# Ends of attention units in pairs, in-place scaling, narrower masks and fused VectorE exponentials in a four-layer attention kernel

## The chip, the cores and the metric

One Trainium2 chip, one of its cores. The metric is the device time of the kernel in microseconds (us), the median of three runs. The engines are TensorE (PE in the profile; PEld is its weight load), VectorE (DVE), ScalarE (ACT), GpSimd (POOL) and SyncE (SP, which here only issues DMAs). PSUM is the memory that TensorE writes: eight banks of 128 x 512 float32.

## The reference, cut to what matters

Four layers on x of 2048 rows by 640 columns. Each normalizes x, projects it to queries, keys and values of 32 heads of 20 columns, and adds attention times an output matrix to x. Layers 0 and 2 (weights A) see a causal window of 256 keys, layers 1 and 3 (weights B) see all 2048 keys.

```python
scores = jnp.einsum("bhqd,bhkd->bhqk", q, k) * (Dh ** -0.5)
scores = jnp.where(mask[None, None], scores, -1e9)     # A: 0 <= q - k < 256; B: no mask
p = _softmax(scores, axis=-1)
o = jnp.einsum("bhqk,bhkd->bhqd", p, v)
...
x = x + _A_ref(_layernorm(x, axis=-1), A_wqkv, A_wo)   # layer 0, then B (1), A (2), B (3)
```

## The kernel before, in words

**Units, banks and tiles.** The queries are cut into four chunks c of 512 rows, the heads into eight groups g of four. A *unit* (layer l, c, g) is the attention of four heads for 512 queries. It consists of *banks*: the scores of one head for 128 keys by 512 queries, one PSUM bank each. A full unit has 16 x 4 = 64 banks, a windowed one 3 x 4 = 12, in which every bank combines parts of two key blocks under one of three masks. The first chunk's units of layers 1 and 3 are cut into parts by key blocks (PARTS, L43), so that they can begin before all keys exist.

**The loop (L1259).** Each turn is a *tile* and advances the planner's clock by one. It takes two to four banks; TensorE writes their scores (L1298) in PSUM banks 0 to 2 at even tiles and 3 to 5 (with 6 at times) at odd ones; ScalarE makes the exponentials of the whole tile in one instruction (L1329) into a tile `pt`; then come pending side tasks (`pump`, L1340), filler matmuls that keep TensorE busy (`keep_clock`, L1342; `unread`, L638, recorded at L640), and the products with the values for tiles two or three turns older (L1363), which accumulate in PSUM bank 7 (`op`). Behind them VectorE gets its share of exponentials (`side_step`, L1385) and the masking of the tile before (L1399): a multiplication by a 0/1 mask, over all 512 columns of a bank, or from the first written block on. Mask 1 has zeros only in the second and third 128 of its 512 columns.

**The side tasks** are generators for projections (L370, L471), layer norms (L394), outputs (`t_out`, L545, matmuls L558) and the units' ends. They are sorted by the unit that needs them; `require` runs them at once when something isn't there in time. Each of them borrows a spare PSUM bank (`take_m`, L269): banks 5 and 6 while tiles are narrow, bank 6 alone after that, at most one borrower a tile.

**A unit's end.** `finish_unit` (L840) copies `op` to a tile `oT` (L863, or L861 with the earlier parts added) and pushes a tail (`t_tail`, L1030), one a unit. Row 20 of each head's 32 rows holds the sum of the exponentials. The tail gathers these sums by four matmuls with a selector (L1044), takes reciprocals (L1049), splits them in two bf16 parts `hl` (L1053, L1054), transposes them on TensorE (L1061), copies that to `rT` (L1063), spreads it over the rows by four matmuls (L1072), and multiplies `oT` by it into the chunk's tile `on` (L1079). Each of the three steps with PSUM borrows the spare bank once. When g = 7 is done, the chunk's output is pushed.

**Packed outputs.** In layer 3 (`packed`, L129) the scaled rows go into one of three staging slots of `on` and are moved by DMAs on SP (L1090) into dense rows, so that the output takes five matmuls for each 128 x 320 block instead of eight. The two last units of the last chunk aren't packed. The output matrix is loaded accordingly, sparse or dense (`load_wop`, L133).

**VectorE's exponentials.** In layers 1 and 3, for c > 0 (two units excepted), the last key block of two heads (layer 1) or four heads (layer 3) is left to VectorE (`aside`, L685). `t_side` (L890) handles two banks as a pair: an eviction each (L911), then ten steps on 1024 columns (L916 to L949) that build 2^x from the bits of the float's exponent and a polynomial of its fraction. Every step has a charge (0.7 or 1.2), and each tile adds a credit (L1384): 1.05 (SIDE_RATE, L40) in the last stage, 0.65 before. A step is issued while the credit is above zero. In the last stage its scores (L904) go to bank 6, at odd tiles (L1266). If a unit closes earlier than its pairs, `side_need` (L980) and `side_done` (L996) force the rest out at once. The products of these banks with the values are L1372.

Of the kernel before, what the change touches and what calls it, by code (L numbers as in the profile page):

```python
# [34 lines left out]
EK, ES, EB, EC, ED = (  # L35
    0.34108128280528366, -0.013389613744261132, 0.7155463694844106,
    0.9531181402314826, 0.010462897723623632,
)
KA = 18
SIDE_RATE = 1.05  # L40
# [9 lines left out]
def kernel(  # L50
# [25 lines left out]
    otp = pool("otp", 3)  # L76
# [22 lines left out]
    spread4 = big.tile([32, 4, P], BF16, name="spread4", tag="spread4")  # L99
# [29 lines left out]
    def packed(l, c):  # L129

        return l > 2

    def load_wop(w, dense):  # L133
        if dense:
            nc.sync.dma_start(out=wop[:, 0:KD, :], in_=wo_in[w].rearrange("(b p) f -> p b f", p=P))
            if w and out_n[0] == 12:
                v = wo_in[w].rearrange("(g j e) f -> j e g f", g=G, j=4)
                for j in range(4):
                    nc.sync.dma_start(
                        out=wop[32 * j : 32 * j + DH, G - 2 : G, :], in_=v[j][:, G - 2 : G, :]  # L140
                    )
            return
        v = wo_in[w].rearrange("(g j e) f -> j e g f", g=G, j=4)
        for j in range(4):
            nc.sync.dma_start(out=wop[32 * j : 32 * j + DH, :, :], in_=v[j])
# [23 lines left out]
    def other_constants():  # L169
        nc.vector.memset(op, 0.0)  # L170
        nc.vector.tensor_copy(
            out=sel4[:], in_=ident[:].rearrange("p (j m) -> p j m", j=4)[:, :, DH]
        )

        sp32 = rzp.tile([32, 2, 16], BF16, name="sp32", tag="sp32")
        nc.vector.tensor_copy(
            out=sp32[:], in_=ident[0:32, 0:32].rearrange("p (n r) -> p n r", n=2)
        )
        sp16 = rzp.tile([32, 16], BF16, name="sp16", tag="sp16")
        nc.vector.tensor_tensor(out=sp16[:], in0=sp32[:, 0, :], in1=sp32[:, 1, :], op=ALU.add)  # L180
        nc.vector.tensor_copy(
            out=spread4[:].rearrange("p q (j m) -> p (q j) m", m=32),
            in_=sp16[:].unsqueeze(2).to_broadcast((32, 16, 32)),
        )
# [360 lines left out]
    def t_out(l, c):  # L545
# [32 lines left out]
        if n < len(out_seq) and (n == 12 or out_seq[n] != out_seq[n - 1]):  # L578
            load_wop(out_seq[n], n >= 12)
# [260 lines left out]
    def finish_unit(u):  # L840
        l, c, g = u.l, u.c, u.g
        if u.part and u.part[1] < NT:
            if not part_o:
                part_o["t"] = big.tile([P, G, C], F32, name="raw_o", tag="early_late")
            raw_o = part_o["t"][:, g, :]
            if u.part[0] == 0:
                nc.vector.tensor_copy(out=raw_o, in_=op)
            else:
                nc.vector.tensor_tensor(out=raw_o, in0=raw_o, in1=op, op=ALU.add)
            return  # L850
        if (l, c) not in ons:
            for ll, cc in list(ons):
                if len(ons) >= 2:
                    require(("out", ll, cc))
            ons[l, c] = onp.tile([P, G, C], BF16, name="on", tag="on")
        on = ons[l, c]
        while len(tails) >= 3:
            require(("tail", *tails[0].name[1:]))
        oT = otp.tile([P, C], BF16, name="oT", tag="oT")
        if u.part:  # L860
            nc.vector.tensor_tensor(out=oT[:], in0=part_o["t"][:, g, :], in1=op, op=ALU.add)  # L861
        else:
            nc.vector.tensor_copy(out=oT[:], in_=op)  # L863
        push_tail(("tail", l, c, g), t_tail(l, c, g, on, oT))


# [4 lines left out]
    def side_start():  # L871

        assert live["xnT"] == 0
        tl = [xtp.tile([P, KD, C], BF16, name="xnT", tag="xnT") for _ in range(4)]
        live["xnT"] += 4
        f = [v[:, 0:4, :].rearrange("p a b -> p (a b)") for v in tl[0:3]]
        side["tiles"] = [v.bitcast(F32) for v in f] + [tl[3][:, 0:2, :].rearrange("p a b -> p (a b)")]
        side["out"] = deque(ka_all[:, KA - 6 + 2 * n : KA - 4 + 2 * n, :] for n in range(3))
        side["late"] = True

    def side_early():

        b = part_o["t"]
        side["tiles"] = [b[:, 2 * n : 2 * n + 2, :].rearrange("p a b -> p (a b)") for n in range(3)]
        side["tiles"].append(b[:, 6, :].bitcast(BF16))
        side["out"] = deque([b[:, 7, :].bitcast(BF16).rearrange("p (a b) -> p a b", a=2)])
        side["gen"] = t_side()
        side_step(False)

    def t_side():  # L890

        V = nc.vector
        while aside:
            u = aside[0]
            for pair in range(len(u.aside) // 2):
                while id(u) not in loaded or (u.l == 3 and not side["late"]):
                    yield None
                for i in range(2):
                    yield "bank"
                    xi, xm, xw, xe = side["tiles"]  # L900
                    if u.l == 3:
# [11 lines left out]
                        scalar1=SCALE * LOG2E * E23, scalar2=127.0 * E23, op0=ALU.mult, op1=ALU.add,  # L913
# [3 lines left out]
                    out=xm.bitcast(I32), in0=xi.bitcast(I32), scalar1=0x7FFFFF, scalar2=0x3F800000,  # L917
# [4 lines left out]
                    out=xi.bitcast(I32), in0=xi.bitcast(I32), scalar1=-0x800000, scalar2=None,  # L922
                    op0=ALU.bitwise_and,
                )
                yield 0.7
                V.tensor_scalar(out=xe, in0=xi, scalar1=0.0, scalar2=None, op0=ALU.max)
                yield 0.7
                V.tensor_scalar(
                    out=xm, in0=xm, scalar1=EK, scalar2=ES, op0=ALU.mult, op1=ALU.add
                )  # L930
                yield 0.7
                V.tensor_tensor(out=xw, in0=xm, in1=xm, op=ALU.mult)
                yield 1.2
                V.tensor_scalar(out=xw, in0=xw, scalar1=EB, scalar2=None, op0=ALU.add)
                yield 0.7
                V.tensor_tensor(out=xw, in0=xw, in1=xw, op=ALU.mult)
                yield 1.2
                V.tensor_scalar(
                    out=xm, in0=xm, scalar1=EC, scalar2=ED, op0=ALU.mult, op1=ALU.add
                )  # L940
                yield 0.7
# [4 lines left out]
                V.tensor_tensor(out=po, in0=xw, in1=xm, op=ALU.add)  # L946
                yield 1.2

                V.tensor_tensor(out=po, in0=po, in1=xe, op=ALU.mult)  # L949
                side_out.setdefault(id(u), []).append(pt)  # L950
                yield 0.7
# [78 lines left out]
    def t_tail(l, c, g, on, oT):  # L1030
        def fill(count):

            for n in range(count * ((l, c, g) == (3, NC - 1, G - 1))):
# [3 lines left out]

        yield ("wait", 2)
# [3 lines left out]
        zp = ps[:, mb, 0:16]  # L1042
        for qb in range(4):
            nc.tensor.matmul(  # L1044
                zp[:, 4 * qb : 4 * qb + 4], lhsT=oT[:, qb * P : (qb + 1) * P],
                rhs=sel4[:], start=True, stop=True,
            )
        rz = rzp.tile([P, 16], F32, name="rz", tag="rz")
        nc.vector.reciprocal(out=rz[:], in_=zp)  # L1049
        drop_m(mb)  # L1050

        hl = rzp.tile([P, 2, 16], BF16, name="hl", tag="hl")
        nc.vector.tensor_copy(out=hl[:, 0, :], in_=rz[:])  # L1053
        nc.vector.tensor_tensor(out=hl[:, 1, :], in0=rz[:], in1=hl[:, 0, :], op=ALU.subtract)  # L1054
# [5 lines left out]
        rp = ps[0:32, mb, :].bitcast(BF16)[:, 0:P]  # L1060
        nc.tensor.transpose(out=rp, in_=hl[:].rearrange("p n r -> p (n r)"), identity=ident[:])  # L1061
        rT = rzp.tile([32, P], BF16, name="rT", tag="rT")
        nc.vector.tensor_copy(out=rT[:], in_=rp)  # L1063
# [3 lines left out]
        yield ("wait", 2 if state["tick"] < last_tick[0] else 1)  # L1067
        mb = yield from take_m()
        warm_bank(mb)
        zb = ps[:, mb, :]  # L1070
        for qb in range(4):
            nc.tensor.matmul(  # L1072
                zb[:, qb * P : (qb + 1) * P], lhsT=spread4[:, qb, :], rhs=rT[:],
                start=True, stop=True,
            )
        end = (l, c) == (3, NC - 1) and g >= G - 2
        spread = packed(l, c) and not end
        nu = on[:, 5 + g % 3 if spread else g, :]
        nc.vector.tensor_tensor(out=nu, in0=oT[:], in1=zb, op=ALU.mult)  # L1079
# [3 lines left out]
        if spread:  # L1083
            yield ("wait", 2)
            for j in range(4):
                r, a = (4 * g + j) * DH, 0
                while a < DH:
# [3 lines left out]
                        out=on[o : o + n, b, :], in_=nu[32 * j + a : 32 * j + a + n, :]  # L1091
# [7 lines left out]
        if g == G - 1:  # L1099
            need = first_use(l + 1, c, 0) if l < 3 else len(units) + c  # L1100
# [85 lines left out]
    with tc.manual_schedule():  # L1186
# [72 lines left out]
        while ended is None or t < ended + 8:  # L1259
# [123 lines left out]
            if n_b:  # L1383
                side["credit"] = min(side["credit"] + (SIDE_RATE if side["late"] else 0.65), 1.2)  # L1384
                side_step(False)  # L1385

            if t > 0 and masked is not None:
                cur_, pt_ = masked
                i = 0
                while i < len(cur_):  # L1390
# [4 lines left out]
                    if m is not None:  # L1395
                        mv_ = masks[:, m, b0 * P :].unsqueeze(1).to_broadcast(
                            (P, k - i, C - b0 * P)
                        )
                        nc.vector.tensor_tensor(  # L1399
                            out=pt_[:, i:k, b0 * P :], in0=pt_[:, i:k, b0 * P :], in1=mv_,  # L1400
                            op=ALU.mult,
# [38 lines left out]
```

## Time and profile before

| what | us |
|---|---|
| median of three runs (2295.11 to 2300.06) | 2298.31 |
| the profiled execution's own time | 2295.7 |
| its span, first to last instruction | 2293.9 |
| ScalarE busy | 2172.7 (95%) |
| TensorE busy | 1981.5 (86%) |
| VectorE busy | 1468.5 (64%) |
| GpSimd busy | 273.2 (12%) |

Up to about 440 us the kernel works on layer 0 and the first parts of layer 1, up to about 1626 us on layers 1 and 2 and the first chunk of layer 3, and then on the other chunks of layer 3. Lines such as L1329 are lines of the kernel. A group of instructions is given with its shapes out<-in, its count, its busy time in us, the mean of one in ns, and the idle time of its engine just before it with what ended that idle time. A wait is given as its total in us, its count and the longest one. TensorE's granted clock is 1.0 or 0.5 at any moment; a mean lies between. Matmuls overlap, so TensorE's busy time isn't its load.

### The profile page before, as it was taken

The page shows a single profiled execution, that of the slowest core. Times are in us where ns is not written, and L with a number is a line of the kernel's source. Part 1 is how long each engine was busy: PE and PEld are TensorE (multiplying, and loading weights), DVE is VectorE, ACT ScalarE, POOL GpSimd, SP SyncE. Part 2 cuts the span into 40 slices and gives each one's busy share as a digit, 9 for nine tenths or more (in the row PEclk, how much of TensorE's full clock was granted, in tenths as well). Part 3 has the DMA queues.
Part 4 walks back from the last instruction along what each step waited for, and adds up shares of the span by engine and source line. Part 5 has one row for each costly group of instructions (what it writes and reads, how often), then busy time and mean ns, then how long its engine had stood idle before and what let it go on. Part 6 is the DMA issues. An engine that isn't in the chain of part 4 may idle for free.

```text
span 2293.9 us, 40624 instructions
## 1 busy us (share of the span) xinstructions
PE 1981.5 (86%) x15618; PEld 709.1 (31%) x15772; DVE 1468.5 (64%) x2736; ACT 2172.7 (95%) x1742; POOL 273.2 (12%) x445
## 2 busy tenths in 40 slices
PE   8889999989889888888888898898878888888887
PEld 3343343333233333233332333333222222222222
DVE  6777776436656666656676644452677877777772
ACT  6789899999999999999899999999999999999997
POOL 4323223200200112001220012002000000000000
PEclk9899999999999999999999999999765565556556
DMA  6223233321310223102330133103211111111100
GB/s 192 76 56 113 71 87 94 96 75 39 90 33 14 59 69 105 30 15 56 85 98 24 27 86 107 33 19 94 70 36 30 31 36 36 30 32 45 38 17 14
DMA packets 88809, 135.25 MB, mean 59 GB/s; under 512 B 21126, under 2 KB 64006, under 8 KB 88614
## 3 DMA queue, kind: packets, MB, share of 16 engines
q1 hardware_dynamic: 69398, 79.47, 13.0%
q0 software_dynamic: 19216, 53.17, 7.9%
q8 instruction: 124, 2.03, 0.4%
q14 instruction: 71, 0.58, 0.1%
HBM read 98.90 MB, written 27.79 MB: 55 GB/s over the span
## 4 chain that ended last, share of the span: by engine, by line
ACT 41%; PE 30%; issue 14%; DVE 13%; DMA 1%; POOL 0%; SPq 0%; ACTq 0%; another core or an unknown queue 0%; DVEq 0%; POOLq 0%
ACT pt L1329 40%; PE ps L1298 7%; PE ps L370 6%; PE ps L1363 5%; PE ps L558 4%; PE ps L471 3%; DVE pt L1399 3%; PE ps L640 2%; DVE st L320 1%; DVE on L1079 1%; DVE raw_o L911 1%; DVE oT L863 1%; ACT ka L1329 1%; PE ps L1292 1%; DVE x_sb L567 1%
## 5 line engine op out<-in xcount | busy, mean ns | idle before, releaser
L1329 ACT ACTIVATE pt<-ps 128x1536 bf16<-128x1536 f32 (+2 forms) x1645 | 2105.8, 1473 | 84.0 <-PE ps L1298 71.0
L1298 PE MATMUL ps<-qt,kt 32*128 32x512 bf16 x4008 | 637.5, 451 | 161.1 <-ACT pt L1329 130.2
L1363 PE MATMUL ps<-pt,vt 128*21 128x512 bf16 x3872 | 465.3, 452 | 5.9 <-issue 3.8
L1298 PEld LDWEIGHTS <-kt 32*128 32x128 bf16 x4008 | 182.5, 93 | 582.9 <-issue 562.6
L1399 DVE TENSOR_TENSOR pt<-pt,masks 128x1024 bf16<-128x1024 bf16 (+5 forms) x403 | 239.5, 626 | 120.9 <-ACT pt L1329 119.9
L640 PE MATMUL ps<-masks,ident 128*128 128x512 bf16 x655 | 228.5, 385 | 35.2 <-DVE rT L1063 9.2
L370 PE MATMUL ps<-xnT,wqk 128*128 128x512 bf16 x765 | 209.0, 384 | 19.1 <-issue 3.2
L1363 PEld LDWEIGHTS <-vt 128*21 128x21 bf16 x3960 | 99.7, 90 | 315.7 <-issue 304.8
L320 DVE CAST st<-ps 128x512 bf16<-128x512 f32 x134 | 92.5, 690 | 162.0 <-PE ps L370 157.5
L558 PE MATMUL ps<-wop,on 128*128 128x320 bf16 x904 | 161.0, 315 | 8.5 <-DVE x_sb L567 4.0
L1298 PE MATMUL ps<-qa,ka 32*128 32x384 bf16 (+2 forms) x1408 | 118.1, 278 | 27.9 <-ACT pt L1329 22.9
L911 DVE TENSOR_SCALAR xnT<-ps 128x512 int32<-128x512 f32 x88 | 60.8, 691 | 109.0 <-PE ps L904 108.8
L1079 DVE TENSOR_TENSOR on<-oT,ps 128x512 bf16<-128x512 bf16 x128 | 87.5, 683 | 55.5 <-PE ps L1072 51.8
L567 DVE TENSOR_TENSOR x_sb<-x_sb,ps 128x320 bf16<-128x320 bf16 x120 | 58.0, 483 | 95.8 <-PE ps L558 95.4
L471 PE MATMUL ps<-wv,xnT 128*128 128x320 bf16 x640 | 109.2, 300 | 8.4 <-DVE va L320 1.8
L863 DVE CAST oT<-ps 128x512 bf16<-128x512 f32 x112 | 76.8, 686 | 57.1 <-PE ps L1363 38.1
L558 PEld LDWEIGHTS <-on 128*128 128x128 bf16 x904 | 81.5, 101 | 74.7 <-issue 46.6
L370 PEld LDWEIGHTS <-wqk 128*128 128x128 bf16 x830 | 70.3, 97 | 109.0 <-issue 51.2
L640 PEld LDWEIGHTS <-ident 128*128 128x128 bf16 x743 | 57.9, 96 | 128.0 <-issue 126.2
L404 POOL TENSOR_SCALAR rstd<-mv 128x4 f32<-128x4 f32 x15 | 5.4, 363 | 740.7 <-DVE mv L391 738.7
L1363 PE MATMUL ps<-pt,va 128*21 128x384 bf16 (+2 forms) x1408 | 77.7, 282 | 4.2 <-DVE pt L1399 2.4
L1298 PEld LDWEIGHTS <-ka 32*128 32x128 bf16 x1408 | 43.2, 92 | 98.0 <-issue 89.4
(109 smaller groups left out, 1820.2 us busy)
## 6 DMA issues: line engine op xcount, KB each, us to landing
vt<-v_d SPq DMA_DIRECT2D x48, 336.0 KB
kt<-k_d SPq DMA_DIRECT2D x192, 80.0 KB
wqk<-in_B_wqkv_dram POOLq DMA_DIRECT2D x80, 160.0 KB, 3.6
wqk<-in_A_wqkv_dram POOLq DMA_DIRECT2D x70, 160.0 KB, 3.5
k_d<-st POOLq DMA_DIRECT2D x75, 128.0 KB, 2.3
q_d<-st POOLq DMA_DIRECT2D x75, 128.0 KB, 2.2
qt<-q_d SPq DMA_DIRECT2D x384, 20.0 KB
v_d<-vs POOLq DMA_DIRECT2D x16, 336.0 KB, 3.0
```

Source lines behind the costliest of these rows:

```text
L320: nc.vector.tensor_copy(out=out_, in_=in_)
L370: nc.tensor.matmul(pq, lhsT=wt[:, dc, :], rhs=xt[:, dc, :], start=(dc == 0), stop=(dc == KD - 1),)
L471: nc.tensor.matmul(pv, lhsT=xt[:, dc, i * P : (i + 1) * P], rhs=wv_sb[l % 2][:, dc, h * HD : (h + 1) * HD], start=(dc == 0), stop=(dc == K ...
L558: nc.tensor.matmul(yp, lhsT=on[:, g, qb * P : (qb + 1) * P], rhs=wop[:, g, i * HD : (i + 1) * HD], start=(g == a), stop=(g == b - 1),)
L640: nc.tensor.matmul(ps[:, b, :], lhsT=ident[:], rhs=masks[:, 0, :], start=True, stop=True)
L863: nc.vector.tensor_copy(out=oT[:], in_=op)
L911: V.tensor_scalar(out=xi.bitcast(I32)[:, i * C : (i + 1) * C], in0=side["psum"], scalar1=SCALE * LOG2E * E23, scalar2=127.0 * E23, op0=ALU ...
L1079: nc.vector.tensor_tensor(out=nu, in0=oT[:], in1=zb, op=ALU.mult)
L1298: nc.tensor.matmul(sp[:, i, col * P : (col + qn) * P], lhsT=u.k(kc, j), rhs=u.q(j, q0, qn), start=True, stop=True,)
L1329: nc.scalar.activation(out=pt[:, i:k, b0 * P :], in_=sp[:, i:k, b0 * P :], func=ACT.Exp, scale=SCALE,)
L1363: nc.tensor.matmul(op[32 * j : 32 * j + VW, q0 * P : (q0 + qn) * P], lhsT=u.v(kc, j), rhs=pg[:, i, col * P : (col + qn) * P], start=(first ...
L1399: nc.vector.tensor_tensor(out=pt_[:, i:k, b0 * P :], in0=pt_[:, i:k, b0 * P :], in1=mv_, op=ALU.mult,)
```

## The change

1. *Ends in pairs.* A tail now serves two units, or one where none is left to pair (behind g = 7, and the two last units of the kernel). One reciprocal, one split and one transpose serve both; the spreading and the scaling are done per unit, one after the other.
2. *In place.* `finish_unit` copies `op` straight to its place in `on` (a staging slot in packed chunks), and the scaling works there. The pool `otp` goes.
3. *Packed* is now layer 3 without chunk 0. The output matrix becomes dense one chunk later.
4. *Masks.* Mask 1 is applied to columns 128 to 383 alone (256 to 383 where the bank starts at block 2).
5. *Exponentials.* The ten steps become six: two on bits and four fused steps (add or multiply, then multiply or add, with a tensor). The charges of a pair fall, and so do the credits, to 0.85 and 0.4. The banks given to VectorE are the same. Three buffers instead of four; two output buffers instead of one in layer 1.

```diff
-SIDE_RATE = 1.05
+SIDE_RATE = 0.85
...
     def packed(l, c):
-        return l > 2
+        return l == 3 and c > 0
...
-        if n < len(out_seq) and (n == 12 or out_seq[n] != out_seq[n - 1]):
-            load_wop(out_seq[n], n >= 12)
+        if n < len(out_seq) and (n == 13 or out_seq[n] != out_seq[n - 1]):
+            load_wop(out_seq[n], n >= 13)
...
-        oT = otp.tile([P, C], BF16, name="oT", tag="oT")
+        end = (l, c) == (3, NC - 1) and g >= G - 2
+        oT = ons[l, c][:, 5 + g % 3 if packed(l, c) and not end else g, :]
...
-        push_tail(("tail", l, c, g), t_tail(l, c, g, on, oT))
+        ended_units.append((l, c, g, oT))
+        if len(ended_units) == 2 or g == G - 1 or end :
+            push_tail(("tail", l, c, g), t_tail(list(ended_units)))
+            ended_units.clear()
...
                     V.tensor_scalar(
                         out=xi.bitcast(I32)[:, i * C : (i + 1) * C], in0=side["psum"],
-                        scalar1=SCALE * LOG2E * E23, scalar2=127.0 * E23, op0=ALU.mult, op1=ALU.add,
+                        scalar1=SCALE * LOG2E * E23, scalar2=-128.0 * E23, op0=ALU.mult, op1=ALU.max,
                     )
...
-                V.tensor_scalar(out=xe, in0=xi, scalar1=0.0, scalar2=None, op0=ALU.max)
-                yield 0.7
-                V.tensor_scalar(
-                    out=xm, in0=xm, scalar1=EK, scalar2=ES, op0=ALU.mult, op1=ALU.add
+                V.scalar_tensor_tensor(
+                    out=xw, in0=xm, scalar=EA, in1=xm, op0=ALU.add, op1=ALU.mult
                 )
-                yield 0.7
-                V.tensor_tensor(out=xw, in0=xm, in1=xm, op=ALU.mult)
                 yield 1.2
...
+                V.scalar_tensor_tensor(
+                    out=po, in0=xw, scalar=ED, in1=xi, op0=ALU.add, op1=ALU.mult
+                )
+                side_out.setdefault(id(u), []).append(pt)
                 yield 1.2
...
+        for i in range(n):
+            yield from scaled(*us[i], 32 * i, rT, fill)
+        if any(packed(l, c) for l, c, g, oT in us):
+            yield ("wait", 2)
+        for u in us:
+            yield from settle(*u)
...
+        nc.vector.tensor_tensor(out=oT, in0=oT, in1=zb, op=ALU.mult)
...
         if g == G - 1:
+            while any(("tail", l, c, n) not in ready for n in range(G)):
+                yield ("wait", 1)
...
-                side["credit"] = min(side["credit"] + (SIDE_RATE if side["late"] else 0.65), 1.2)
+                side["credit"] = min(side["credit"] + (SIDE_RATE if side["late"] else 0.4), 1.2)
...
+                        cols = slice(max(b0, m == 1) * P, 3 * P if m == 1 else C)
```

In the pair's tail the reciprocals stand side by side (32 columns), the split has 64, and `rT` 64 rows, of which the second unit's spreading reads rows 32 to 63; `spread4` is made for 64 rows.

More of the change, by code (lines that the diff above doesn't have):

```diff
@@ L34 @@
 LOG2E = 1.4426950408889634
[L35 to L38, printed above, removed]
+EA, EB, EC, ED = -0.10468731, 1.17604568, 0.83196789, 0.24582313
 KA = 18
-SIDE_RATE = 1.05
+SIDE_RATE = 0.85
 QA = 4
@@ L75 @@
     ptp = pool("ptp", 6)
-    otp = pool("otp", 3)
     stp = pool("stp", 4)
@@ L98 @@
     sel4 = big.tile([P, 4], BF16, name="sel4", tag="sel4")
-    spread4 = big.tile([32, 4, P], BF16, name="spread4", tag="spread4")
+    spread4 = big.tile([64, 4, P], BF16, name="spread4", tag="spread4")
     masks = big.tile([P, 3, C], BF16, name="masks", tag="masks")
@@ L135, in load_wop @@
             nc.sync.dma_start(out=wop[:, 0:KD, :], in_=wo_in[w].rearrange("(b p) f -> p b f", p=P))
[L136 to L141, printed above, removed]
             return
@@ L173, in other_constants @@
         )
[L175 to L184, printed above, removed]
+        sp32 = rzp.tile([64, 2, 16], BF16, name="sp32", tag="sp32")
+        sp16 = rzp.tile([64, 16], BF16, name="sp16", tag="sp16")
+        for u in range(2):
+            r = slice(32 * u, 32 * u + 32)
+            nc.vector.tensor_copy(
+                out=sp32[r], in_=ident[r, r].rearrange("p (n r) -> p n r", n=2)
+            )
+            nc.vector.tensor_tensor(
+                out=sp16[r], in0=sp32[r, 0, :], in1=sp32[r, 1, :], op=ALU.add
+            )
+            nc.vector.tensor_copy(
+                out=spread4[r].rearrange("p q (j m) -> p (q j) m", m=32),
+                in_=sp16[r].unsqueeze(2).to_broadcast((32, 16, 32)),
+            )
     ready = set()
@@ L855, in finish_unit @@
             ons[l, c] = onp.tile([P, G, C], BF16, name="on", tag="on")
-        on = ons[l, c]
         while len(tails) >= 3:
-            require(("tail", *tails[0].name[1:]))
-        oT = otp.tile([P, C], BF16, name="oT", tag="oT")
+            require(tails[0].name)
+        end = (l, c) == (3, NC - 1) and g >= G - 2
+        oT = ons[l, c][:, 5 + g % 3 if packed(l, c) and not end else g, :]
         if u.part:
-            nc.vector.tensor_tensor(out=oT[:], in0=part_o["t"][:, g, :], in1=op, op=ALU.add)
+            nc.vector.tensor_tensor(out=oT, in0=part_o["t"][:, g, :], in1=op, op=ALU.add)
         else:
-            nc.vector.tensor_copy(out=oT[:], in_=op)
-        push_tail(("tail", l, c, g), t_tail(l, c, g, on, oT))
+            nc.vector.tensor_copy(out=oT, in_=op)
+        ended_units.append((l, c, g, oT))
+        if len(ended_units) == 2 or g == G - 1 or end :
+            push_tail(("tail", l, c, g), t_tail(list(ended_units)))
+            ended_units.clear()
+    ended_units = []
     aside = deque(u for u in units if u.aside)
@@ L873, in side_start @@
         assert live["xnT"] == 0
-        tl = [xtp.tile([P, KD, C], BF16, name="xnT", tag="xnT") for _ in range(4)]
-        live["xnT"] += 4
+        tl = [xtp.tile([P, KD, C], BF16, name="xnT", tag="xnT") for _ in range(3)]
+        live["xnT"] += 3
         f = [v[:, 0:4, :].rearrange("p a b -> p (a b)") for v in tl[0:3]]
-        side["tiles"] = [v.bitcast(F32) for v in f] + [tl[3][:, 0:2, :].rearrange("p a b -> p (a b)")]
+        side["tiles"] = [v.bitcast(F32) for v in f]
         side["out"] = deque(ka_all[:, KA - 6 + 2 * n : KA - 4 + 2 * n, :] for n in range(3))
@@ L884, in side_early @@
         side["tiles"] = [b[:, 2 * n : 2 * n + 2, :].rearrange("p a b -> p (a b)") for n in range(3)]
-        side["tiles"].append(b[:, 6, :].bitcast(BF16))
-        side["out"] = deque([b[:, 7, :].bitcast(BF16).rearrange("p (a b) -> p a b", a=2)])
+        side["out"] = deque(
+            b[:, n, :].bitcast(BF16).rearrange("p (a b) -> p a b", a=2) for n in (6, 7)
+        )
         side["gen"] = t_side()
@@ L899, in t_side @@
                     yield "bank"
-                    xi, xm, xw, xe = side["tiles"]
+                    xi, xm, xw = side["tiles"]
                     if u.l == 3:
@@ L916, in t_side @@
                 V.tensor_scalar(
-                    out=xm.bitcast(I32), in0=xi.bitcast(I32), scalar1=0x7FFFFF, scalar2=0x3F800000,
+                    out=xm.bitcast(I32), in0=xi.bitcast(I32), scalar1=0x7FFFFF, scalar2=0x3E800000,
                     op0=ALU.bitwise_and, op1=ALU.bitwise_or,
@@ L921, in t_side @@
                 V.tensor_scalar(
-                    out=xi.bitcast(I32), in0=xi.bitcast(I32), scalar1=-0x800000, scalar2=None,
-                    op0=ALU.bitwise_and,
+                    out=xi.bitcast(I32), in0=xi.bitcast(I32), scalar1=0x7F800000,
+                    scalar2=0x40000000, op0=ALU.bitwise_and, op1=ALU.bitwise_xor,
                 )
                 yield 0.7
-                V.tensor_scalar(out=xe, in0=xi, scalar1=0.0, scalar2=None, op0=ALU.max)
-                yield 0.7
-                V.tensor_scalar(
-                    out=xm, in0=xm, scalar1=EK, scalar2=ES, op0=ALU.mult, op1=ALU.add
-                )
-                yield 0.7
-                V.tensor_tensor(out=xw, in0=xm, in1=xm, op=ALU.mult)
+                V.scalar_tensor_tensor(
+                    out=xw, in0=xm, scalar=EA, in1=xm, op0=ALU.add, op1=ALU.mult
+                )
                 yield 1.2
-                V.tensor_scalar(out=xw, in0=xw, scalar1=EB, scalar2=None, op0=ALU.add)
-                yield 0.7
-                V.tensor_tensor(out=xw, in0=xw, in1=xw, op=ALU.mult)
+                V.scalar_tensor_tensor(
+                    out=xm, in0=xw, scalar=EB, in1=xm, op0=ALU.mult, op1=ALU.add
+                )
                 yield 1.2
-                V.tensor_scalar(
-                    out=xm, in0=xm, scalar1=EC, scalar2=ED, op0=ALU.mult, op1=ALU.add
+                V.scalar_tensor_tensor(
+                    out=xw, in0=xw, scalar=EC, in1=xm, op0=ALU.add, op1=ALU.mult
                 )
-                yield 0.7
+                yield 1.2
                 while not side["out"]:
@@ L945, in t_side @@
                 po = pt.rearrange("p a b -> p (a b)")
-                V.tensor_tensor(out=po, in0=xw, in1=xm, op=ALU.add)
+                V.scalar_tensor_tensor(
+                    out=po, in0=xw, scalar=ED, in1=xi, op0=ALU.add, op1=ALU.mult
+                )
+                side_out.setdefault(id(u), []).append(pt)
                 yield 1.2
-                V.tensor_tensor(out=po, in0=po, in1=xe, op=ALU.mult)
-                side_out.setdefault(id(u), []).append(pt)
-                yield 0.7
             aside.popleft()
@@ L1028, in pv_emitted, with t_tail @@
             live["va"] -= 2 + 2 * (u.c > 0) + 2 * (u.c == NC - 1)
-    def t_tail(l, c, g, on, oT):
+    def t_tail(us):
+        final = us[-1][0:3] == (3, NC - 1, G - 1)
         def fill(count):
-            for n in range(count * ((l, c, g) == (3, NC - 1, G - 1))):
+            for n in range(count * final):
                 nc.tensor.matmul(
@@ L1036, in fill @@
                 )
+        n = len(us)
         yield ("wait", 2)
@@ L1041, in t_tail @@
         warm_bank(mb)
[L1042 to L1049, printed above, removed]
+        zp = ps[:, mb, 0 : 16 * n]
+        for i, (l, c, g, oT) in enumerate(us):
+            for qb in range(4):
+                a = 16 * i + 4 * qb
+                nc.tensor.matmul(
+                    zp[:, a : a + 4], lhsT=oT[:, qb * P : (qb + 1) * P],
+                    rhs=sel4[:], start=True, stop=True,
+                )
+        rz = rzp.tile([P, 2, 16], F32, name="rz", tag="rz")[:, 0:n, :]
+        nc.vector.reciprocal(out=rz.rearrange("p u r -> p (u r)"), in_=zp)
         drop_m(mb)
-        hl = rzp.tile([P, 2, 16], BF16, name="hl", tag="hl")
-        nc.vector.tensor_copy(out=hl[:, 0, :], in_=rz[:])
-        nc.vector.tensor_tensor(out=hl[:, 1, :], in0=rz[:], in1=hl[:, 0, :], op=ALU.subtract)
+        hl = rzp.tile([P, 2, 2, 16], BF16, name="hl", tag="hl")[:, 0:n]
+        nc.vector.tensor_copy(out=hl[:, :, 0, :], in_=rz)
+        nc.vector.tensor_tensor(out=hl[:, :, 1, :], in0=rz, in1=hl[:, :, 0, :], op=ALU.subtract)
         yield ("pe", 0.25)
@@ L1059, in t_tail @@
         warm_bank(mb)
[L1060 to L1063, printed above, removed]
+        rp = ps[0 : 32 * n, mb, :].bitcast(BF16)[:, 0:P]
+        nc.tensor.transpose(
+            out=rp, in_=hl.rearrange("p u n r -> p (u n r)"), identity=ident[:]
+        )
+        rT = rzp.tile([64, P], BF16, name="rT", tag="rT")
+        nc.vector.tensor_copy(out=rT[0 : 32 * n], in_=rp)
         drop_m(mb)
@@ L1067, in t_tail, with scaled @@
         yield ("wait", 2 if state["tick"] < last_tick[0] else 1)
+        for i in range(n):
[4 more added lines that the diff above has]
+            yield from settle(*u)
+    def scaled(l, c, g, oT, r, rT, fill):
         mb = yield from take_m()
@@ L1072, in t_tail @@
             nc.tensor.matmul(
-                zb[:, qb * P : (qb + 1) * P], lhsT=spread4[:, qb, :], rhs=rT[:],
-                start=True, stop=True,
-            )
[L1076 to L1079, printed above, removed]
+                zb[:, qb * P : (qb + 1) * P], lhsT=spread4[r : r + 32, qb, :],
+                rhs=rT[r : r + 32, :], start=True, stop=True,
+            )
+        nc.vector.tensor_tensor(out=oT, in0=oT, in1=zb, op=ALU.mult)
         drop_m(mb)
@@ L1082, in t_tail, with settle @@
         fill(3)
-        if spread:
-            yield ("wait", 2)
+    def settle(l, c, g, oT):
+        on = ons[l, c]
+        if packed(l, c) and not ((l, c) == (3, NC - 1) and g >= G - 2):
             for j in range(4):
@@ L1090, in t_tail @@
                     nc.sync.dma_start(
-                        out=on[o : o + n, b, :], in_=nu[32 * j + a : 32 * j + a + n, :]
+                        out=on[o : o + n, b, :], in_=oT[32 * j + a : 32 * j + a + n, :]
                     )
@@ L1395 @@
                     if m is not None:
-                        mv_ = masks[:, m, b0 * P :].unsqueeze(1).to_broadcast(
-                            (P, k - i, C - b0 * P)
+                        cols = slice(max(b0, m == 1) * P, 3 * P if m == 1 else C)
+                        mv_ = masks[:, m, cols].unsqueeze(1).to_broadcast(
+                            (P, k - i, cols.stop - cols.start)
                         )
                         nc.vector.tensor_tensor(
-                            out=pt_[:, i:k, b0 * P :], in0=pt_[:, i:k, b0 * P :], in1=mv_,
-                            op=ALU.mult,
+                            out=pt_[:, i:k, cols], in0=pt_[:, i:k, cols], in1=mv_, op=ALU.mult
                         )
```

## The prediction

> **What bounds the kernel now.** I read the page's busy line first, then busy time by stage, the waits of ScalarE (ACT) by stage, the chain of waits in the worst stretch, and the groups of instructions by shape.
>
> The busy line, the three stages, the stretch 90 to 126 us, and one slice of the last stage:
>
> ```profile
> PE 1981.5 (86%) x15618; PEld 709.1 (31%) x15772; DVE 1468.5 (64%) x2736; ACT 2172.7 (95%) x1742; POOL 273.2 (12%) x445
> ...
> 0.00:300.00 300.00, 267.58 (x2409) 115.32 (x2441) 219.96 (x519) 243.50 (x271) 95.04 (x174) 0.96 0.35 103
> 300.00:1626.00 1326.00, 1166.05 (x9750) 446.12 (x9870) 763.25 (x1501) 1281.62 (x999) 178.20 (x272) 1.00 0.23 62
> 1626.00:2294.00 668.00, 547.90 (x3465) 147.61 (x3461) 485.28 (x718) 647.55 (x474) 0.00 (x0) 0.56 0.11 33
> ...
> 90.00:126.00 36.00, 27.81 (x269) 12.94 (x272) 31.32 (x80) 21.20 (x19) 5.13 (x7) 0.76 0.17 48
> ...
> 1700.00:1800.00 100.00, 83.00 (x509) 20.51 (x505) 75.72 (x107) 100.00 (x74) 0.00 (x0) 0.50 0.12 34
> ```
>
> The columns are PE, PEld, DVE, ACT, POOL (busy us and instructions), then TensorE's granted clock. ScalarE's exponentials fill the span. It is idle 56.5 us of the first 300, 44.4 us up to 1626, and 20.5 us after, of which some 11.4 us lie behind its last exponential (about 2282.5 us). In the last stage it has no gap: 74 exponentials in 100.00 us, 1.35 us each. The change leaves ScalarE's columns as they are, so all that can be gained is part of 121 us of idle time, and most of that is early.
>
> ScalarE's waits from 0 to 300 us, then 300 to 1626, then behind 1626:
>
> ```profile
> ACT pt L1329 <- PE ps L1298: 24.9, 39, 4.4
> ...
> ACT pt L1329 <- PE ps L1298: 37.3, 91, 1.6
> ...
> ACT pt L1329 <- PE ps L1298: 8.7, 16, 1.2
> ```
>
> ScalarE always waits for TensorE's scores. What delays TensorE differs. From 90 to 126 us, above, VectorE is busy 31.32 of 36 us, ScalarE only 21.20, and the clock is 0.76; of those 36 us the masks (L1399) take 13.30, and they lead the chain of waits with 32%. The clock stands at 0.5 from 46.3 to 53.2 and from 94.1 to 111.2 us; the first drop follows a wait of TensorE for VectorE (`on`, L1079) of 2.15 us. In the middle stage TensorE waits for VectorE in many small pieces, most of them where its filler (L640) wants the one spare PSUM bank that VectorE still reads:
>
> ```profile
> PE ps L640 <- DVE rT L1063: 9.2, 17, 1.2
> ...
> PE ps L640 <- DVE st L320: 6.3, 15, 0.9
> PE ps L640 <- DVE on L1079: 5.2, 14, 0.8
> ```
>
> **The parts, and what each costs.** Durations are from these groups:
>
> ```profile
> L1399 DVE TENSOR_TENSOR pt<-pt,masks 128x1024 bf16<-128x1024 bf16 x132 | 89.2, 683 | 30.5 <-ACT pt L1329 30.1
> L1399 DVE TENSOR_TENSOR pt<-pt,masks 128x1536 bf16<-128x1536 bf16 x86 | 81.4, 950 | 44.0 <-ACT pt L1329 43.5
> L932 DVE TENSOR_TENSOR xnT<-xnT 128x1024 f32<-128x1024 f32 x40 | 48.8, 1220 | 0.6
> L916 DVE TENSOR_SCALAR xnT<-xnT 128x1024 int32<-128x1024 int32 x40 | 27.7, 694 | 1.3
> L949 DVE TENSOR_TENSOR ka<-ka,xnT 128x1024 bf16<-128x1024 bf16 x39 | 26.9, 688 | 0.9
> L558 PE MATMUL ps<-wop,on 128*128 128x320 bf16 x40 | 10.5, 416 | 0.3 <-DVE on L1079 0.2
> ```
>
> *Exponentials on VectorE.* A pair of banks now takes two evictions of 0.69, six one-source steps (0.69 each), three float products of 1.22 and a bf16 product of 0.69: 9.9 us. Afterwards: two evictions, two one-source steps, four fused steps. The trace has no large fused step. From below it costs 0.69 (the two-source bf16 row), from above 1.91 (a one-source step and a product in turn). I take 1.22, the row of the two-source float product, which it is nearest to. The pair then costs 1.38 + 1.39 + 4.88 = 7.65 us (5.5 to 10.4). For 68 pairs (88 + 48 evictions at L911, halved) VectorE gives back 151 us. Almost none of it is on the path. 44 pairs lie in the last stage, where ScalarE has no gap. Their pace in tiles doesn't change: the planner's charges are 9.9 at 1.05 a tile, then 7.6 at 0.85, 9.4 and 8.9 tiles; since a bank is taken at odd tiles alone, both become 10, and two pairs fill a unit's 20 tiles. The cover is ScalarE's own 20 x 1.35 us a unit; without it the closing matmuls (L1372) would wait up to one fused step, 1.22 us x 23 units = 28 us. In the middle stage 9.9 / 0.65 = 15 tiles become 7.6 / 0.4 = 19, still within the unit's 21 (62 banks by three, two tiles short by one). The third input buffer freed and a second output buffer only loosen this.
>
> *Masks.* From the two mask rows a column costs (950 - 683) / 512 = 0.52 ns. The middle mask loses 256 columns in 192 banks and 128 in 64: 57,344 columns, 30 us, an eighth of the 239.5 us. From 90 to 126 us that is 13.3 / 8 = 1.7 us on the path.
>
> *Tails in pairs.* Per pair one reciprocal, two hl steps and one rT copy go (0.255 + 0.184 + 0.175 + 0.208 = 0.82 us of VectorE, less some 0.05 for wider ones), and one transpose on TensorE (0.24 us). The eight selecting and eight spreading matmuls and both scalings stay. Over some 62 pairs: 48 us of VectorE, 15 us of TensorE. Six turns of the spare bank become four. The first unit of a pair is held until the second ends; nobody needs it, since the output waits for the eighth unit, which closes a pair at once. The new wait there finds all earlier tails done. VectorE in all: 1468 - 151 - 30 - 48 = 1239 us.
>
> *In place.* The eviction (L863) writes straight into `on`, so it comes behind the output matmuls of two chunks before, and in packed chunks behind the DMAs of three units before. Both end tens of us earlier; otherwise a wait of about one eviction, 0.7 us a unit. On SP a pair's DMAs come together: five took 3.6 us, so ten hold the next unit's loads 3.6 us longer, of a unit of 27 us. Hidden; beyond that each us counts once a pair.
>
> *Chunk 0 of layer 3 unpacked.* Eight matmuls per output group instead of five, 24 more. A group, once begun, goes out within one tile. At half clock their spacing in the trace is 0.275 us (five in 1.45 us), so each group grows by 0.83 us, 6.6 us in all. Today ScalarE is idle 3.0 us in the 36 us around it (1644 to 1680), in about four of eight groups; these can hide nothing more: +3 us (0 at full clock and with room, 6.6 if all is exposed). Its strip DMAs on SP disappear, off the path.
>
> **Where the gain is.** Early: 90 to 126 us, masks 1.7 and tails 1.3 (half of the 2.7 us that its reciprocals, hl and rT take), and perhaps a clock window less: 4 us (0 to 12). The wait of 2.15 us at 43 us, for a scaling that now comes a unit later, disappears: ScalarE's stalls behind it were 2.6, 1.5 and 1.1 us, of which I take 4 (0 to 5). Twelve transposes x 0.23 = 2.8 us of a TensorE that is nine tenths busy; half reaches ScalarE: 1.5. Sum 9.5. Middle: the rT waits halve (4.6 of 9.2 us); the others shrink with VectorE's load (masks 18, exponentials 53, tails 32 of 763: 13.5% of 11.5 = 1.6). About half of that 6.2 us reaches ScalarE: 3 (-3, if the longer fused steps sit before a bank's reader, to 8). Late: -3. Net 9.5 + 3 - 3 = 9.5 us.
>
> [...] Or both early drops vanish: that would give 5 + 12 there, not 8. But in the second drop VectorE remains the chain, and in the middle the planner adds fillers for what falls away. I take the rows.
>
> **The rivals.** (1) *The early drops vanish whole*: early 5 + 12 + 1.5, middle 5, late -2: -21.5 us, 2277. For it: both follow VectorE's jam. Against: the layer norm's statistics, 20% of that chain, stay. Chance 0.13. (2) *VectorE is off the path*: what it gives back is idle time, the early gain is some 4 us and the unpacked output eats it: 2297. For it: VectorE is busy 64% and ScalarE 95%. Against: the 31.32 us above. Chance 0.24. (3) *Slower by the unpacked output*: all eight groups run at half clock and expose their 0.83 us, +6.6, with nothing kept early because TensorE's order of work binds there: 2305. It decides once the other gains are under 2 us. Against: before it, some groups ran at full clock. Chance 0.14. That the change doesn't do as it says (the pace slower than planned, exponentials forced out at a unit's end) would show as waits at L1372; the tile counts speak against it, and it is in (3)'s share.
>
> **The numbers.** The profiled execution took 2295.7 us (span 2293.9), 2.6 under the median 2298.3; the saving is taken from the median: 2298.3 - 9.5 = 2289. Forecast 0.49. About 0.2% (4.6 us) is what this measurement can tell from no change. Faster: 0.49 + 0.13 = 0.62, same 0.24, slower 0.14. The range, 2276 to 2302, takes in most of (1), all of (2) and the lower part of (3).
>
> **What would show it.** ScalarE's busy time and its 1.35 us each stay. VectorE near 1240 us and fused steps of 1.22 us; 1.9 would overthrow the first part. The stretch 90 to 126 us has ScalarE busy over 24 us. The clock doesn't fall near 46 us. L640's waits for rT halve. Around the unpacked output ScalarE's idle time rises from 3 to about 6 us. I am wrong if the first 300 us keep their 56 us of idle time, or if new waits stand at L1372 or L863.

## The result, and the profile after

The changed kernel takes 2284.79 us (median of four runs, 2283.59 to 2287.35), against 2298.72 us before in the same comparison. The ratio is 0.9943 (95% interval 0.9926 to 0.9961): 13 us saved of some 2298, with 9 to 17 inside the interval. The profiled execution took 2284.0 us, 11.7 less than that of before.

The busy line of the page after, then busy time by stage, the stretch from 90 to 126 us, one from 40 to 55, and a slice of the last stage (columns PE, PEld, DVE, ACT, POOL, then the clock):

```profile
PE 1978.4 (87%) x15586; PEld 704.1 (31%) x15746; DVE 1272.2 (56%) x2214; ACT 2169.6 (95%) x1741; POOL 271.0 (12%) x445
...
0.00:300.00 300.00, 269.46 (x2444) 114.77 (x2476) 206.36 (x476) 248.88 (x277) 96.13 (x177) 0.97 0.36 106
300.00:1626.00 1326.00, 1172.52 (x9752) 445.51 (x9878) 684.28 (x1256) 1288.04 (x1004) 174.87 (x269) 0.99 0.22 62
...
90.00:126.00 36.00, 31.29 (x294) 13.97 (x296) 30.36 (x77) 22.92 (x21) 5.19 (x7) 0.75 0.13 37
...
40.00:55.00 15.00, 11.35 (x112) 4.85 (x114) 13.24 (x36) 10.98 (x19) 7.06 (x9) 1.00 0.35 97
1700.00:1800.00 100.00, 82.96 (x513) 20.13 (x511) 59.39 (x72) 99.97 (x74) 0.00 (x0) 0.50 0.11 32
```

ScalarE's busy time is the same to 3 us, and so is its pace at the end (74 exponentials in 100 us). VectorE has lost 196 us of work, and the last stage doesn't notice it: 59 us busy of 100 there instead of 76. What changed is ScalarE's idle time: 51.1 us instead of 56.5 in the first 300 us, 38.0 instead of 44.4 up to 1626 us.

Those are windows of fixed times, and the second holds more work after the change. The 128 evictions at the units' ends come in the same order in every version, so each can be compared with its counterpart. The 24th and the 104th (the end of the early and of the middle stage), before and then after:

```profile
285.80 0.68 DVE L863 CAST oT<-ps 128x512 bf16<-128x512 f32 x1
1625.42 0.68 DVE L861 TENSOR_TENSOR oT<-raw_o,ps 128x512 bf16<-128x512 f32 x1
...
280.44 0.68 DVE L857 CAST on<-ps 128x512 bf16<-128x512 f32 x1
1608.75 0.69 DVE L855 TENSOR_TENSOR on<-raw_o,ps 128x512 bf16<-128x512 f32 x1 [2.73 <-PE ps L1373]
```

So the change is 5.4 us ahead after the early stage and 16.7 us at the end of the middle one, which is therefore 11.3 us shorter; the last stage gives back 5.1 us. In the middle stage ScalarE is idle 8.8 us less and busy 2.5 us less.

Of VectorE's groups after, the fused step and the reciprocal of a pair:

```profile
L925 DVE SCALAR_TENSOR_TENSOR xnT<-xnT 128x1024 f32<-128x1024 f32 x44 | 53.6, 1218 | 0.0
...
L1048 DVE RECIPROCAL rz<-ps 128x32 f32<-128x32 f32 x63 | 22.4, 356 | 36.5 <-PE ps L1043 35.3 <-ACT va L312 0.8
```

The fused step costs 1.22 us, as the float product does. The reciprocal of 32 columns takes 0.356 us against 0.255 for 16.

### The profile page after: what moved, and what is told of

Read it like the earlier page. It is cut to its first block, busy times and chain, and to the rows that moved or that the text cites. A ratio compares the mean times of both kernels' runs of the same rounds, so it can differ in the third digit from the quotient of the medians.

```text
span 2282.3 us, 40030 instructions
## 1 busy us (share of the span) xinstructions
PE 1978.4 (87%) x15586; PEld 704.1 (31%) x15746; DVE 1272.2 (56%) x2214; ACT 2169.6 (95%) x1741; POOL 271.0 (12%) x445
## 4 chain that ended last, share of the span: by engine, by line
ACT 45%; PE 30%; issue 16%; DVE 9%; DMA 0%; ACTq 0%; POOL 0%; SPq 0%; DVEq 0%; POOLq 0%
ACT pt L1339 44%; PE ps L1308 7%; PE ps L364 6%; PE ps L552 5%; PE ps L1373 4%; PE ps L465 3%; DVE pt L1410 2%; PE ps L634 1%; DVE st L314 1%; DVE on L1085 1%; ACT ka L1339 1%; PE ps L1081 1%; DVE x_sb L561 1%; PE ps L429 0%; DVE raw_o L910 0%
## 5 line engine op out<-in xcount | busy, mean ns | idle before, releaser
L1410 DVE TENSOR_TENSOR pt<-pt,masks 128x1024 bf16<-128x1024 bf16 (+6 forms) x403 | 209.5, 554 | 151.0 <-ACT pt L1339 150.5
L634 PE MATMUL ps<-masks,ident 128*128 128x512 bf16 x708 | 243.5, 387 | 27.7 <-DVE on L1085 7.1
L1085 DVE TENSOR_TENSOR on<-on,ps 128x512 bf16<-128x512 bf16 x128 | 86.4, 685 | 65.8 <-PE ps L1081 64.7
L857 DVE CAST on<-ps 128x512 bf16<-128x512 f32 x112 | 77.1, 688 | 75.1 <-PE ps L1373 48.3
```

The costliest lines, as they stand in the source:

```text
L634: nc.tensor.matmul(ps[:, b, :], lhsT=ident[:], rhs=masks[:, 0, :], start=True, stop=True)
L857: nc.vector.tensor_copy(out=oT, in_=op)
L1085: nc.vector.tensor_tensor(out=oT, in0=oT, in1=zb, op=ALU.mult)
L1410: nc.vector.tensor_tensor(out=pt_[:, i:k, cols], in0=pt_[:, i:k, cols], in1=mv_, op=ALU.mult)
```

## The experiments

The change was taken apart into masks (M), fused exponentials with their pace (X), and pairs with in-place scaling (P). All combinations ran. Each time is beside runs of the kernel before on the same chip.

**Masks alone.**

```diff
...
+                        cols = slice(max(b0, m == 1) * P, 3 * P if m == 1 else C)
...
```

> The kernel before with the narrower middle mask alone (30 us less of VectorE's time, nothing else moved; TensorE's order of work is the same). Theory A, VectorE's queue is on the path early: 3 to 5 us faster, all of it in the first 300 us, with ScalarE busier from 90 to 126 us. Theory B, the gain comes from TensorE's order of work (fewer turns of the spare bank) and VectorE's time is idle time anyway: within 1 us of before. Theory C, what counts is whether the clock drops fall away: several us at once if the drop at 46 or at 94 us is gone, else nothing.

Measured: 2293.87 us, ratio 0.9982 (0.9968 to 0.9997), 4 us saved. ScalarE's idle time in the first 300 us falls to 51.2 us, as far as in the whole change:

```profile
0.00:300.00 300.00, 270.04 (x2456) 116.50 (x2490) 212.09 (x525) 248.82 (x276) 96.36 (x176) 0.97 0.36 106
300.00:1626.00 1326.00, 1170.87 (x9720) 446.78 (x9841) 745.82 (x1497) 1279.53 (x997) 176.46 (x269) 0.99 0.22 62
```

So VectorE's queue is on the path early (theory A). At the 24th unit's end this version is 5.4 us ahead, as the whole change is: the masks alone can account for the early gain. (In the stretch from 90 to 126 us, though, ScalarE is busy only 0.5 us more; and the half clock near 46 us lasts 3.4 us instead of 6.9, so part of the gain may come by way of the clock.)

**Fused exponentials and their pace alone.**

```diff
-SIDE_RATE = 1.05
+SIDE_RATE = 0.85
...
+                V.scalar_tensor_tensor(
+                    out=xw, in0=xm, scalar=EA, in1=xm, op0=ALU.add, op1=ALU.mult
+                )
```

> The kernel before with the fused exponentials and their lower pace alone (151 us less of VectorE's time, all behind 600 us). Theory A: 1 to 3 us faster, from the middle stage (600 to 1626 us); nothing in the last stage, where ScalarE has no gap. Theory B: within 1 us. If the longer fused steps hold up readers of the spare bank: up to 3 us slower.

Measured: 2298.24 us, ratio 0.9996 (0.9981 to 1.0012): no difference. VectorE is busy 1332.0 us instead of 1468.5, and nothing comes of it by itself.

**Pairs and in-place scaling alone, outputs packed as before.** (This version and the next change the output of layer 3's chunk 0, whose staging slots are reused before they are free: in the next version's trace the fourth unit's eviction stands at 1579.9 us and the DMAs out of the same slot from 1584.3 us on. They are read for their times.)

```diff
-        push_tail(("tail", l, c, g), t_tail(l, c, g, on, oT))
+        ended_units.append((l, c, g, oT))
+        if len(ended_units) == 2 or g == G - 1 or end :
```

> The kernel before with ends in pairs and in-place scaling alone; masks, exponentials and packed outputs (layer 3, chunk 0 too) as before. Theory A: 5 to 8 us faster, early and in the middle, the clock drop at 46 us gone. Theory B: 10 to 16 us faster, that is all of the change's gain and the 3 us that the unpacked output costs. Theory C: the amount goes with the number of clock drops before 1600 us.

Measured: 2310.94 us, ratio 1.0068 (1.0046 to 1.0091): 13 us slower by the medians. Theories A and B both fall in this form. Its trace has six drops of the clock between 300 and 1570 us, where before has two.

**The kernel after with layer 3's chunk 0 packed again.**

```diff
-        return l == 3 and c > 0
+        return l > 2
```

> The kernel after with layer 3's chunk 0 packed again (five matmuls instead of eight for its output, its strip DMAs back). All theories agree on the sign if the unpacked output costs what was predicted: 3 us faster than the kernel after, ScalarE's idle time around that output back from 6 to 3 us. If its eight matmuls hide in TensorE's slack: no difference from after.

Measured: 2287.56 us, ratio 0.9956 (0.9940 to 0.9971). The 3 us forecast didn't come; the interval takes in the kernel after (0.9943), so neither a gain nor a loss is shown. One of TensorE's waits from 1560 to 1620 us, and VectorE's instruction behind it in the timeline:

```profile
PE ps L640 <- DVE on L1091: 4.6, 1, 4.6
...
1592.56 0.69 DVE L861 TENSOR_TENSOR on<-raw_o,ps 128x512 bf16<-128x512 f32 x1 [6.59 <-DMA on<-on]
```

The eviction of a unit waits 6.59 us for the DMAs that empty its staging slot, since the units there end about every 7 us (in the kernel before, their eight evictions run from 1574.8 to 1625.4 us). The scaling that TensorE waits for stands behind it on VectorE and starts at 1593.16 us, late too, and TensorE stands for 4.6 us. In the kernel after, without packing, the same 60 us have no idle time of ScalarE, here 5.9 us. The price of the unpacked output is there as well: between its first and last matmul (1622 to 1664 us) ScalarE is idle 5.5 us, where the 36 us around the output before held 3.0. Measured against the kernel before by the units' ends, the packed version's lead falls from 17.1 us at the 96th to 9.7 at the 104th; the kernel after keeps 16.7, but loses 3.6 of it up to the 112th, where the packed version wins 1.6. Most of the two costs cancels.

**Masks and exponentials without pairs.**

> Masks and fused exponentials on the kernel before, ends still one unit at a time and into a tile of their own. Theory D, formed from the runs so far: the pairs bunch VectorE's and TensorE's work and lose time by themselves; what gains is VectorE's shorter queue. Then this version is at least as fast as the kernel after, 10 to 14 us faster than before. Theory E, the parts need each other (pairs take turns of the spare bank and TensorE's work away, but only pay where VectorE's queue is short): 3 to 6 us faster than before, that is the sum of the masks' 4 us and the exponentials' 0.

Measured: 2292.81 us, ratio 0.9964 (0.9943 to 0.9985). By the medians that is 5.5 us, in theory E's bounds; by the ratio it is 8 us with an interval of 3 to 13, which doesn't exclude theory D. Whether the pairs add anything is not shown by it: the intervals of this version and of the kernel after (0.9926 to 0.9961) overlap. The single runs reach from 2283.26 us, as fast as the kernel after, to 2304.91, while all twelve runs of the two versions that have the pairs as well, packed or not, lie between 2283.21 and 2289.43.

**Pairs, in place and unpacked, old masks and exponentials.**

> The kernel after with the old exponentials (and their pace) and the old masks: pairs, in-place scaling and the unpacked output of layer 3's chunk 0. The run with pairs alone lost 13 us, but with the packed output, whose staging slots units of five tiles write over. If that packing made the loss: within 3 us of before. If the pairs make it (theories D and E): 6 to 13 us slower than before.

Measured: 2310.96 us, ratio 1.0047 (1.0030 to 1.0065). So it is the pairs that lose by themselves, not the packing.

**Pairs and masks; pairs and exponentials.**

> The kernel after with the old ten-step exponentials and their pace. Theory E with the masks as what pairs need: 5 to 10 us faster than before. If pairs need the lighter exponentials: no faster than before, up to 6 us slower.

> The kernel after with the old, full-width mask 1. If pairs need the lighter exponentials: 6 to 10 us faster than before. If they need the lighter masks: no faster than before. The early stage (0 to 300 us) has no exponentials on VectorE, so the masks' share there is seen directly: ScalarE's idle time of the first 300 us back at 55 us.

Measured: 2297.99 us, ratio 0.9987 (0.9973 to 1.0002), and 2297.88 us, ratio 0.9991 (0.9976 to 1.0007). In both the expected gain failed to come. The effect of the pairs goes from +0.47% (alone) over +0.05% (with masks) and -0.05% (with exponentials) to -0.21% (with both). That the loss goes away with either companion is clear of noise; that a gain is left with both is not (each ratio's interval is about 0.2% to either side).

In the table, ScalarE's idle time is that of the windows, the half-clock time is between 300 and 1570 us, and the last column is the time gained on the kernel before between the 24th and the 96th unit's end (285.8 to 1502.0 us there; a minus is time lost):

| version | ratio | idle 0-300 | idle 300-1626 | at half clock | gained, ends 24 to 96 |
|---|---|---|---|---|---|
| before | 1 | 56.5 | 44.4 | 6.8 | 0 |
| M | 0.9982 | 51.2 | 46.5 | 13.7 | 1.4 |
| X | 0.9996 | 56.7 | 47.3 | 17.1 | -3.2 |
| P | 1.0047 | 55.1 | 53.0 | 30.7 | -8.2 |
| M X | 0.9964 | 52.3 | 46.2 | 20.5 | -0.4 |
| P M | 0.9987 | 49.4 | 48.3 | 27.3 | -2.6 |
| P X | 0.9991 | 56.7 | 47.2 | 20.5 | -0.2 |
| P M X (after) | 0.9943 | 51.1 | 38.0 | 0.0 | 11.3 |
| P M X, packed | 0.9956 | 51.1 | 42.1 | 0.0 | 11.9 |

The last four columns are of one profiled execution each, and the clock drops differ from run to run. In the first 300 us all versions with the narrow masks are near 51 us, all others near 56. In the middle stage only the two versions with all three parts stand out, by 11 to 12 us, and they alone have no clock drop there. But the profiled execution of M X took 2294.24 us, and three of its twelve runs took 2283 to 2284 us at a mean clock of 0.865 to 0.867; there is no trace of these. So it may be that the pairs only make usual what at times happens without them.

What stood ahead of a drop in the kernel before (the clock is 0.5 from 551.5 to 554.9 us):

```profile
548.72 1.20 DVE L932 TENSOR_TENSOR raw_o<-raw_o 128x1024 f32<-128x1024 f32 x1
549.85 0.20 DVE L1063 COPY rT<-ps 32x128 bf16<-32x128 bf16 x1
...
550.11 0.38 PE L640 MATMUL ps<-masks,ident 128*128 128x512 bf16 x1 [1.04 <-DVE rT L1063]
```

A product of the exponentials (1.20 us) stands in front of the copy of `rT`, and a filler matmul waits 1.04 us for the bank that the copy reads. With pairs and the old masks and exponentials (clock 0.5 from 822.6 us):

```profile
821.32 1.21 DVE L937 TENSOR_TENSOR raw_o<-raw_o 128x1024 f32<-128x1024 f32 x1
822.45 0.48 DVE L317 CAST vs<-ps 128x320 bf16<-128x320 f32 x1
...
822.98 0.58 PE L637 MATMUL ps<-masks,ident 128*128 128x512 bf16 x1 [1.59 <-DVE vs L317]
```

The same pattern, with another eviction behind the product. In that stage of that version TensorE's fillers wait less for `rT` (1.7 us instead of 9.2) but more for other things, the scaling first:

```profile
PE ps L637 <- DVE on L1092: 6.4, 16, 1.0
...
PE ps L637 <- DVE vs L317: 4.4, 5, 1.8
```

In the kernel after only two of TensorE's waits for VectorE between 300 and 1570 us are over 0.8 us (eleven before, seven with pairs alone, eight with masks and exponentials alone). This suggests how pairs and exponentials help each other. Without pairs, about half of these long waits are for `rT`. Pairs with the old exponentials replace them by three waits of 1.6 to 1.9 us, longer than any before (1.16), and keep these three with the narrow masks too. Pairs with the fused exponentials have neither kind: two waits over 0.8 us, with the old masks or the new.

That the drops go with the time is seen in one and the same program: twelve runs of masks and exponentials lie between 2283.26 us (mean clock 0.867) and 2304.91 us (0.852), with a correlation of -0.95 and 1.48 us for each 0.001 of the mean clock. 0.001 is 4.6 us at half clock, so each us at half clock goes with 0.32 us of time. Of the kernel before, 25 and 30 runs give 1.30 and 1.24 us for each 0.001 (correlation -0.91). The kernel after has a clock of 0.864 in all four runs.

**What stays open.** No run changed the clock and left the rest; more fillers, and more columns for VectorE now that it has room, were not tried. That the drops cause the middle stage's difference is therefore argued from the correlation and the table, not shown alone; a slow course could also bring the drops. Nor is it shown what the masks add in the middle stage: pairs with exponentials have the same two waits over 0.8 us as the kernel after, and yet four drops and no gain there.

## Why the prediction was right or wrong

**The sum** held: 9.5 us predicted, 13 measured (9 to 17). It held in part by luck. Early, middle and late were put at 9.5, 3 and -3 us; by the units' ends they are 5.4, 11.3 and -5.1 us in the profiled executions, and the errors cancel.

**What bounds the kernel** held. ScalarE's work is the same to 3 us, and most of the gain is idle time of the first and middle stages.

**VectorE's share.** The masks gave 30 us (239.5 to 209.5), the fused step took 1.22 us, both as worked out. The exponentials gave 136 us by their own run, not 151: the page's busy time counts the overlap of neighbours once, and the sum of the means counted it twice (added one by one, VectorE's durations do fall by 151.5 us in that run). The tails gave 43 by their groups' busy times instead of 48 (105 to 62 us for reciprocal, hl and rT), the term for wider instructions being too small: the pair's reciprocal alone is 0.10 us longer. In all VectorE fell to 1272 us, not 1239.

**The last stage** held: exponentials there gain nothing, the pace in tiles is the same, and no wait at L1372's successor (L1382) appears on TensorE.

**Early: 9.5 predicted, 5.4 measured, and not by the parts named.** The step that failed is the share of the tails. The drop at 46 us disappeared as forecast, yet ScalarE gained only 1.6 us from 40 to 55 us (10.98 busy instead of 9.37), not 4: another wait, of TensorE for a scaling (1.9 us), stands there now. From 90 to 126 us it gained 1.7 us, not 4, and stays under the 24 us named; the half clock there still lasts 17 us. Its size is that of the masks' 1.7 us, but the masks' own run gained only 0.5 us in this stretch, so the two shares can't be told apart there. Pairs alone leave 55.1 of 56.5 us.

**Middle: 3 predicted, 6.4 less idle time in the fixed window, 11.3 us gained by the units' ends,** outside the step's range (-3 to 8). The `rT` waits didn't halve; they almost vanished as fillers' waits (9.2 to 0.5 us). But the reasoning added the parts up, each by its share, and this is the step that was wrong in kind: the three alone give -0.18, -0.04 and +0.47%, which sums to a loss, and the whole gives -0.57%. Pairs were put down as 2.8 us of TensorE and half of the `rT` waits gained; alone they cost 11 us by the ratio (13 by the medians), 8 of them in the middle stage. "The planner adds fillers for what falls away" was also too simple, for a filler can itself wait for VectorE, and the two drops shown came behind waits of 1.04 and 1.59 us.

**The unpacked output** cost 2.5 us of ScalarE's time where 3 were forecast; by the units' ends (104th to 112th) the kernel after loses 3.6 us. Behind the last unit's end another 1.4 us are lost, for which the prediction had no term. The remark that an in-place eviction finds its slot empty "tens of us earlier" holds for the units of 20 tiles that the change leaves packed. With chunk 0's short units it does not, as the version packed again showed.

**The rivals.** That VectorE is off the path is refuted by the masks' run. The whole disappearance of the early drops did not happen. The slower rival named the wrong mechanism: a loss was possible, by pairs meeting a long queue on VectorE. The prediction set the first drop behind a wait of 2.15 us; in the 3.41 us ahead of that drop TensorE was busy 1.26 us, 37% (last section).

## What to carry to other kernels

Where an engine with idle time reads a buffer that the busy engine's partner waits for, look at its queue and not at its busy share alone (30 us less of VectorE's masks brought 4 us here, 136 us less of its exponentials none); take parts of a change apart in all combinations before crediting one of them. Work that is bunched to save instructions can lose more in a long queue than it saves (pairs ran at 1.0047 of the time before alone, at 0.9943 with both companions). A buffer that is reused in place must be empty at the shortest period of its users, not at the usual one (units that ended every 7 us made an eviction wait 6.59 us).

## What the runs showed of the hardware

One unchanged program (masks and exponentials, twelve runs) ran from 2283.26 to 2304.91 us with its mean granted clock between 0.867 and 0.852.

In the trace of the kernel before, half clock up to 1600 us lasted 6.83 us (from 46.34 us), 17.07 (from 94.13), 3.41 (from 551.52) and 3.41 (from 920.16); in that of the kernel after, 17.07 (from 91.03) and 3.41 (from 125.16). All are one, two or five times 3.413 us, so the traces are read here in windows of that length, counted forward and back from the first drop of each. The windows with TensorE's longest wait for a scaling near 46 us, one before and two after, with the columns as above:

```profile
42.93:46.34 3.41, 1.26 (x13) 0.58 (x9) 3.31 (x12) 1.30 (x2) 2.50 (x4) 1.00 0.52 137
...
46.66:50.07 3.41, 2.07 (x20) 1.03 (x21) 3.38 (x9) 2.32 (x3) 3.33 (x5) 1.00 0.18 38
50.07:53.48 3.41, 2.41 (x23) 0.96 (x23) 3.29 (x9) 1.00 (x2) 0.76 (x1) 1.00 0.44 126
```

In the kernel before, the wait of 2.15 us lies within one window, TensorE is busy 1.26 of its 3.41 us, and the next window has half clock. In the kernel after, a wait of 1.85 us lies in two windows (0.85 and 1.01 us), TensorE is busy 2.07 and 2.41 us (61 and 71%), and the clock stays at 1.0. In the windows ahead of the six drops TensorE was busy for 37, 46, 62 and 65% (before) and 52 and 49% (after). The first 1600 us of these two traces have 911 other windows at full clock, from 9 us on, where the clock's records begin; in none of them was TensorE busy for less than 55%, in 65 for 55 to 75%. So the busy share sets the four early drops apart from the rest, but not the two of the middle stage; what decided there is open.
